# A scheduled attention and MoE kernel: one operand of the weight conversion moves to PSUM, three small steps change engine, the planner gets other costs

## The chip, the core and the metric

The kernel runs on one core of one Trainium2 chip, in one launch. The metric is the device time of one execution in microseconds (us). Engines are named as in the profile: PE is TensorE, DVE VectorE, ACT ScalarE, POOL GpSimd, SP the SyncE queue that issues the DMAs.

## What is computed

Three steps in a row, in float32 (the weights arrive as float64):

```python
for t in range(S):                     # gated linear attention, B=4, H=8, S=768, D=48
    state = alpha[:, :, t, :, None] * state + einsum('bhd,bhe->bhde', k[:, :, t], v[:, :, t])
    y[:, :, t] = einsum('bhd,bhde->bhe', q[:, :, t], state)
x = y.transpose(0, 2, 1, 3).reshape(3072, 384)
h = x @ w_in                           # 384 -> 2048
g = (a0 + a1*h + a2*h**2 + a3*h**3) / (1 + |b0|*|h| + |b1|*h**2 + 1e-6)
x = g @ w_out                          # 2048 -> 384
s = x @ w_gate                         # 384 -> 1536
out = (s / (1 + exp(-s)) * (x @ w_val)) @ w_out2
```

## The kernel before, in words

**Stages.** Attention goes over 24 chunks of 128 time steps (`attention`). For a chunk PE transposes alpha, k and q (aT, kT, qT), DVE runs two scans along time over alpha (bb forward, cc backward, lines 666 and 674) and makes kt and qt from them (682, 692), PE makes the scores sc, ACT copies them to aa and POOL masks them (715). PE transposes kt back (kn), and forms the state's update upd and the output yT from aa, v and the carried state st_s. The state st_c is then multiplied by bC, the products of alpha at the chunk's end (678, 781, 783), and ACT copies it into st_s (788). The result goes to DRAM (xd).

The first MoE (`moe1`) takes 512 tokens at a time and 16 slices f of w_in and w_out. A slice is an **h group** of nine matmuls, a chain over ACT, POOL and DVE (lines 863 to 893) that ends in gg, and nine second matmuls into acc. t2, an affine function of |h|, has two lines: 867 for ACT and 869 for DVE. The second MoE (`moe2`) takes 384 tokens and 12 slices: gate pg, value pv, their product pp, and the output matmuls po. Each float32 product is three fp32r matmuls of a high part and a low part.

**Conversion.** Each of the 68 weight slices arrives as two 32-bit words per number (`split_`). DVE shifts the upper word (line 550, result e), joins the sign to it (556, result x), ACT scales the lower word (578) and copies x to the high part (580), POOL adds the lower word (583) and subtracts the high part (531). The slices 1 to 6 of a fixed list do the last steps on DVE (564 to 574). e and a later temporary share one SBUF tile.

**Order.** Nothing of the order stands in the code: each step is given to `Plan.op` with a due time, one or two engines with a cost in us, what it reads and writes, and a mark for DVE steps that the planner keeps apart from POOL's. `Plan.order` plays the plan through, in cost and due time, and the instructions are issued in the order that comes out. A step with two engines gets the second one only where the plan is late by more than a threshold:

```python
            if c[2]:
                r = max(r, c[0] + late - THETA)
```

PSUM has eight banks, which the planner hands out; three belong to the accumulators, the others to h, the transposes (tr), attention's scores and outputs (att), and the gate and value groups (g). While an h group holds one:

```python
                    if held["h"] + held["tr"] + held["att"] + held["g"] + len(t) > 5:
                        return 1e9
```

An h bank is held until line 889 has read it, since the chain writes intermediate results back into it.

Of the kernel before, what the change touches and what calls it, by code (L numbers as in the profile page):

```python
# [19 lines left out]
PE, DVE, ACT, POOL, DMA = range(5)  # L20
CAPS = {"w": 99, "early": 9, "att": 3, "h": 5, "acc": 3, "g": 4, "tr": 1}
HOP = {PE: 0.22, DVE: 0.2, ACT: 0.2, POOL: 0.15, DMA: 2.1}
SAME = {PE: 0.0, DVE: 0.07, ACT: 0.09, POOL: 0.05, DMA: 2.1}
THETA = 4.46

# [9 lines left out]
class Plan:  # L35
# [51 lines left out]
    def order(self):  # L87
# [46 lines left out]
        def ready(e, c):  # L134
            r = c[3]
            if c[2]:
                r = max(r, c[0] + late - THETA)
            if e == DVE and c[4]:
                r = max(r, lock[1])
            if e == POOL:  # L140
                r = max(r, lock[0])
            if takes[c[1]]:
                t = takes[c[1]]
                us = units[t[0].cls]
                if len(us) < len(t) or held[t[0].kind] + len(t) > CAPS[t[0].kind]:
                    return 1e9
                if t[0].cls == "bank" and t[0].kind != "acc" and (held["h"] or t[0].kind == "h"):
                    if held["h"] + held["tr"] + held["att"] + held["g"] + len(t) > 5:
                        return 1e9
                r = max(r, sorted(us.values())[len(t) - 1])  # L150
            return r
# [203 lines left out]
def gla_moe_moe2_kernel(  # L355
# [151 lines left out]
    def split_(v, name, src):  # L507
# [18 lines left out]

        plan.op(v - 4.14, [(DMA, 1.1 if wide else 0.6, load)], (), (st,))

        def low(x):
            def f(eng):  # L530
                return lambda: eng.tensor_tensor(w.t[:, 1], x.t, w.t[:, 0].bitcast(F32), ALU.subtract)  # L531

            plan.op(v, ways(0.96, f(nc.gpsimd), 0.47, f(nc.vector)), (x, w), (w,))

        if not wide:
            plan.op(v, [(ACT, 0.42, lambda: nc.scalar.copy(w.t[:, 0], st.t))], (st,), (w,))
            low(st)
            return w
        e = new("stage", [128, DM], F32, "we", 2, name + "_e")
        x = new("stage", [128, DM], F32, "wx", 2, name + "_x")  # L540

        def w0():
            return st.t[:, :, 0]

        def w1():
# [3 lines left out]
            v,  # L549
            [(DVE, 0.27, lambda: nc.vector.tensor_scalar(  # L550
                e.t.bitcast(U32), w1(), 5, 2, ALU.logical_shift_left, ALU.logical_shift_right), True)],
            (st,), (e,),
# [3 lines left out]
            [(DVE, 0.47, lambda: nc.vector.scalar_tensor_tensor(  # L556
                x.t.bitcast(U32), w1(), 0xC0000000, e.t.bitcast(U32), ALU.bitwise_and, ALU.bitwise_or), True)],
            (st, e), (x,),
        )
        if slots_dve[0] <= slots[0] <= slots_dve[1]:  # L560
            plan.op(v, [(ACT, 0.42, lambda: nc.scalar.copy(w.t[:, 0], x.t))], (x,), (w,))
            plan.op(
                v,
                [(DVE, 0.27, lambda: nc.vector.tensor_scalar(
                    e.t.bitcast(U32), x.t.bitcast(U32), 0xFF800000, None, ALU.bitwise_and))],
                (x,), (e,),
            )
            plan.op(
                v,
                [(DVE, 0.47, lambda: nc.vector.scalar_tensor_tensor(  # L570
                    e.t, w0(), 2.0**-52, e.t, ALU.mult, ALU.mult), True)],
                (st, e), (e,),
            )
            plan.op(v, [(DVE, 0.47, lambda: nc.vector.tensor_tensor(x.t, x.t, e.t, ALU.add))], (x, e), (x,))
        else:


            plan.op(v, [(ACT, 0.5, lambda: nc.scalar.activation(e.t.bitcast(U32), w0(), AF.Copy, scale=2.0**-29))],
                    (st,), (e,))
            plan.op(v, [(ACT, 0.42, lambda: nc.scalar.copy(w.t[:, 0], x.t))], (x,), (w,))  # L580
            plan.op(
                v,
                [(POOL, 0.96, lambda: nc.gpsimd.tensor_tensor(
                    x.t.bitcast(U32), x.t.bitcast(U32), e.t.bitcast(U32), ALU.add))],
                (x, e), (x,),
            )
# [43 lines left out]
    def attention(v0, dv, m):  # L630
# [76 lines left out]
        for g in range(2):  # L707
            plan.op(
                v0 + 4 * dv,
                [(ACT, 0.48, lambda g=g: nc.scalar.copy(aa[g].t, quad(sc[g].t)))],  # L710
                (sc[g],), (aa[g],),
            )
            plan.op(
                v0 + 4 * dv,
                [(POOL, 0.6, lambda g=g: nc.gpsimd.affine_select(
                    out=aa[g].t, in_=aa[g].t, pattern=[[0, NP], [1, 128]], compare_op=ALU.is_ge,
                    fill=0.0, base=0, channel_multiplier=-1))],
                (aa[g],), (aa[g],),
            )
# [57 lines left out]
        if first:  # L777
            plan.op(v0 + 6 * dv, [(DVE, 0.27, lambda: nc.vector.tensor_tensor(st_c.t, u4(), bCx(), ALU.mult))],
                    (upd, bC), (st_c,))
        else:  # L780
            plan.op(v0 + 6 * dv, [(DVE, 0.27, lambda: nc.vector.tensor_tensor(st_c.t, u4(), st_c.t, ALU.add))],
                    (upd, st_c), (st_c,))
            plan.op(v0 + 6 * dv, [(DVE, 0.27, lambda: nc.vector.tensor_tensor(st_c.t, st_c.t, bCx(), ALU.mult))],
                    (st_c, bC), (st_c,))
# [53 lines left out]
    def moe1(vs, n, part, f0, f1, xt, win, wout):  # L838
# [4 lines left out]
        def first(f):  # L843
# [9 lines left out]
            def mm1():  # L853
                for j in range(NJ):
# [178 lines left out]
    def moe2(vs, n, f0, f1, yy, wg, wv, wo):  # L1033
# [28 lines left out]
        def second(f, pp):  # L1062
# [167 lines left out]
```

## Time and profile before

| | |
|---|---|
| three runs | 1053.42 to 1054.92 us, median 1054.92 |
| profiled execution: its time, its span | 1056.59 us, 1054.9 us |
| mean granted PE clock | 0.985 of full |
| busy: PE, DVE, ACT, POOL | 1002.8, 841.2, 614.5, 460.4 us |
| HBM traffic over the span | 107 GB/s |

The span is the time from the first instruction to the last; the execution's own time is a little longer. An engine's busy time is the time in which it had an instruction in work; that of a DVE or POOL instruction includes what it waits for a port inside the instruction. PE's matmuls overlap each other, so that the difference of their starts is their price, not their length. Attention lies between 0 and 440 us, the first MoE's h groups between 53 and 573 us, the second MoE behind them.

### The profile page before, as it was taken

The page shows a single profiled execution, that of the slowest core. Times are in us where ns is not written, and L with a number is a line of the kernel's source. Part 1 is how long each engine was busy: PE and PEld are TensorE (multiplying, and loading weights), DVE is VectorE, ACT ScalarE, POOL GpSimd, SP SyncE. Part 2 cuts the span into 40 slices and gives each one's busy share as a digit, 9 for nine tenths or more (in the row PEclk, how much of TensorE's full clock was granted, in tenths as well). Part 3 has the DMA queues.
Part 4 walks back from the last instruction along what each step waited for, and adds up shares of the span by engine and source line. Part 5 has one row for each costly group of instructions (what it writes and reads, how often), then busy time and mean ns, then how long its engine had stood idle before and what let it go on. Part 6 is the DMA issues. An engine that isn't in the chain of part 4 may idle for free.

```text
span 1054.9 us, 16741 instructions
## 1 busy us (share of the span) xinstructions
PE 1002.8 (95%) x5974; PEld 898.5 (85%) x5974; DVE 841.2 (80%) x1570; ACT 614.5 (58%) x1148; POOL 460.4 (44%) x397
## 2 busy tenths in 40 slices
PE   8799889999799999999999999999999999999996
PEld 7677677788578788878887888999999999999996
DVE  7999999999998988987999888659866756565422
ACT  4585687998688988788898665432222213232221
POOL 3365778878785775556787765500000000000000
PEclk9999999999999999999999999999999999999999
DMA  8885754422432222031012454224545444343100
GB/s 187 198 205 130 175 143 113 128 83 76 113 86 80 81 67 81 1 112 44 1 61 61 136 174 148 83 81 130 172 142 166 150 120 152 105 141 106 53 1 26
DMA packets 163883, 113.64 MB, mean 108 GB/s; under 512 B 105040, under 2 KB 141904, under 8 KB 163792
## 3 DMA queue, kind: packets, MB, share of 16 engines
q1 hardware_dynamic: 163792, 112.49, 38.3%
q8 instruction: 49, 0.80, 0.3%
q14 instruction: 42, 0.34, 0.1%
HBM read 95.95 MB, written 16.52 MB: 107 GB/s over the span
## 4 chain that ended last, share of the span: by engine, by line
PE 34%; DVE 9%; ACT 3%; DMA 2%; issue 2%; POOL 0%; DVEq 0%; SPq 0%; ACTq 0%
PE po L1069 4%; PE po L1068 4%; PE po L1067 4%; PE pg L834 4%; PE pv L835 4%; PE pg L836 4%; PE pg L835 4%; PE pv L836 4%; PE pv L834 4%; DVE yy L950 1%; DMA out_dram<-os 1%; DVE h L885 1%; DVE t L883 1%; DMA wg_st<-in_moe_w_gate_dram 1%; DVE t L879 1%
## 5 line engine op out<-in xcount | busy, mean ns | idle before, releaser
L877 POOL TENSOR_TENSOR t<-t,t 128x512 f32<-128x512 f32 x96 | 130.4, 1359 | 70.8 <-ACT t L867 54.9
L804 POOL TENSOR_TENSOR gg<-t,gg 128x512 fp32r<-128x512 f32 x96 | 134.3, 1401 | 55.3 <-ACT gg L893 33.4
L1053 ACT CAST pp<-sg 128x384 fp32r<-128x384 f32 x96 | 49.2, 513 | 176.2 <-DVE sg L1051 169.3
L1051 DVE TENSOR_TENSOR sg<-sg,pv 128x384 f32<-128x384 f32 x96 | 53.0, 552 | 105.0 <-PE pv L836 103.6
L834 PE MATMUL acc<-gg,wout 128*128 128x512 f32 x288 | 117.3, 407 | 4.1 <-DVE ys L924 2.5
L834 PE MATMUL h<-xt,win 128*128 128x512 f32 x288 | 117.0, 406 | 2.8 <-ACT aa L710 2.1
L835 PE MATMUL acc<-gg,wout 128*128 128x512 f32 x288 | 114.9, 399 | 3.6 <-POOL gg L804 3.5
L836 PE MATMUL h<-xt,win 128*128 128x512 f32 x288 | 114.0, 396 | 3.4 <-POOL win L531 1.8
L835 PE MATMUL h<-xt,win 128*128 128x512 f32 x288 | 114.0, 396 | 0.1
L836 PE MATMUL acc<-gg,wout 128*128 128x512 f32 x288 | 114.0, 396 | 0.0
L1050 ACT ACTIVATE sg<-pg 128x384 f32<-128x384 f32 x96 | 47.1, 491 | 90.8 <-PE pg L836 89.5
L1069 PE MATMUL po<-wo,pp 128*128 128x384 f32 x288 | 98.4, 342 | 1.6 <-DVE pp L1056 1.6
L1067 PE MATMUL po<-wo,pp 128*128 128x384 f32 x288 | 97.4, 338 | 2.1 <-ACT pp L1053 2.0
L835 PE MATMUL pg<-yy,wg 128*128 128x384 f32 x288 | 97.1, 337 | 0.9 <-DVE yy L950 0.9
L1068 PE MATMUL po<-wo,pp 128*128 128x384 f32 x288 | 97.3, 338 | 0.0
L834 PE MATMUL pg<-yy,wg 128*128 128x384 f32 x288 | 97.1, 337 | 0.0
L836 PE MATMUL pg<-yy,wg 128*128 128x384 f32 x288 | 96.9, 337 | 0.0
L835 PE MATMUL pv<-yy,wv 128*128 128x384 f32 x288 | 96.7, 336 | 0.0
L836 PE MATMUL pv<-yy,wv 128*128 128x384 f32 x288 | 96.5, 335 | 0.0
L834 PE MATMUL pv<-yy,wv 128*128 128x384 f32 x288 | 96.4, 335 | 0.0
L883 DVE SCALAR_TENSOR_TENSOR t<-t,h 128x512 f32<-128x512 f32 x96 | 65.3, 680 | 21.4 <-ACT h L882 17.2
L1056 DVE TENSOR_TENSOR pp<-sg,pp 128x384 fp32r<-128x384 f32 x96 | 60.2, 627 | 26.7 <-ACT pp L1053 25.6
(143 smaller groups left out, 2648.0 us busy)
## 6 DMA issues: line engine op xcount, KB each, us to landing
chk<-in_moe_w_out_dram SPq DMA_DIRECT2D x28, 384.0 KB, 3.3
xr<-xd SPq DMA_DIRECT2D x27, 256.0 KB, 2.8
y1d<-ys SPq DMA_DIRECT2D x27, 256.0 KB, 2.2
win_st<-in_moe_w_in_dram SPq DMA_DIRECT2D x16, 384.0 KB, 3.5
wout_st<-in_moe_w_out_dram SPq DMA_DIRECT2D x16, 384.0 KB, 3.6
chk<-in_moe_w_in_dram SPq DMA_DIRECT2D x16, 384.0 KB, 3.8
nata<-in_alpha_dram SPq DMA_DIRECT2D x24, 192.0 KB, 3.4
natk<-in_k_dram SPq DMA_DIRECT2D x24, 192.0 KB, 3.1
```

The lines of the kernel that those rows point to most:

```text
L804: return lambda: eng.tensor_tensor(out_(), in0(), in1().bitcast(F32), ALU.subtract)
L834: nc.tensor.matmul(out_, wh, xh, start=start, stop=False)
L835: nc.tensor.matmul(out_, wh, xl, start=False, stop=False)
L836: nc.tensor.matmul(out_, wl, xh, start=False, stop=stop)
L877: plan.op(v, [pool(T, lambda: nc.gpsimd.tensor_tensor(t1(), t1(), t2(), ALU.mult))], (b1, b2), (b1,))
L883: plan.op(v, [dve(T, lambda: nc.vector.scalar_tensor_tensor(t1(), t1(), ONE_EPS, h(), ALU.add, ALU.mult))], (b1, hb), (b1,))
L1051: plan.op(v, [(DVE, 0.47, lambda: nc.vector.tensor_tensor(sg.t, sg.t, pv.t[:, 0:TB], ALU.mult))], (sg, pv), (sg,))
L1053: plan.op(v, [(ACT, 0.42, lambda: nc.scalar.copy(pp.t[:, 0], sg.t))], (sg,), (pp,))
L1056: [(DVE, 0.47, lambda: nc.vector.tensor_tensor(pp.t[:, 1], sg.t, pp.t[:, 0].bitcast(F32), ALU.subtract))],
L1067: nc.tensor.matmul(o, pp.t[:, 0, s], w[:, 0], start=f == f0, stop=False)
L1068: nc.tensor.matmul(o, pp.t[:, 0, s], w[:, 1], start=False, stop=False)
L1069: nc.tensor.matmul(o, pp.t[:, 1, s], w[:, 0], start=False, stop=f == f1 - 1)
```

## The change

- The conversion's e moves from SBUF to a PSUM bank of a new kind, cv, of which one may be held at a time and which counts among the five. The later temporary r gets the SBUF tile. Lines 550 and 556 (554 and 560 in the new file) lose the mark that keeps them apart from POOL; two of the steps of slices 1 to 6 get or lose it.
- bC is copied by ACT; the state's product with bC goes to POOL; the second engine for t2 is POOL for DVE.
- The planner's costs, biases, due times and threshold get other values (DMA of a weight 1.5 for 1.1, POOL's steps some 4% more, the output matmuls' due time 5.98 for 4.32 behind the gate group, an attention chunk PA 7.59 for 6.93 and others). The order of all engines comes out anew.

```diff
-CAPS = {"w": 99, "early": 9, "att": 3, "h": 5, "acc": 3, "g": 4, "tr": 1}
+CAPS = {"w": 99, "early": 9, "att": 3, "h": 5, "acc": 3, "g": 4, "tr": 1, "cv": 1}
-THETA = 4.46
+THETA = 3.82
...
-                    if held["h"] + held["tr"] + held["att"] + held["g"] + len(t) > 5:
+                    if held["h"] + held["tr"] + held["att"] + held["g"] + held["cv"] + len(t) > 5:
...
-        e = new("stage", [128, DM], F32, "we", 2, name + "_e")
+        e = bank("cv", name + "_e")
+        r = new("stage", [128, DM], F32, "we", 2, name + "_r")
...
-            [(DVE, 0.27, lambda: nc.vector.tensor_scalar(
-                e.t.bitcast(U32), w1(), 5, 2, ALU.logical_shift_left, ALU.logical_shift_right), True)],
+            [(DVE, 0.45, lambda: nc.vector.tensor_scalar(
+                ex().bitcast(U32), w1(), 5, 2, ALU.logical_shift_left, ALU.logical_shift_right))],
...
-                x.t.bitcast(U32), w1(), 0xC0000000, e.t.bitcast(U32), ALU.bitwise_and, ALU.bitwise_or), True)],
+                x.t.bitcast(U32), w1(), 0xC0000000, ex().bitcast(U32), ALU.bitwise_and, ALU.bitwise_or))],
...
-        plan.op(v0, [(DVE, 0.08, lambda: nc.vector.tensor_copy(bC.t, bb.t[:, C:L:C1]))], (bb,), (bC,))
+        plan.op(v0, [(ACT, 0.1, lambda: nc.scalar.copy(bC.t, bb.t[:, C:L:C1]))], (bb,), (bC,))
...
-            plan.op(v0 + 6 * dv, [(DVE, 0.27, lambda: nc.vector.tensor_tensor(st_c.t, st_c.t, bCx(), ALU.mult))],
+            plan.op(v0 + 6 * dv, [(POOL, 0.57, lambda: nc.gpsimd.tensor_tensor(st_c.t, st_c.t, bCx(), ALU.mult))],
...
-                    (DVE, 0.19 + T / 1920, lambda: nc.vector.tensor_scalar(
+                    (POOL, 0.17 + T * 0.001, lambda: nc.gpsimd.tensor_scalar(
                         t2(), t1(), absb[:, 1:2], absb[:, 0:1], ALU.mult, ALU.add)),
...
-            plan.op(vs[f - f0] + 4.32, [(PE, 1.56, mm4)], (wo[f], pp), tuple(po))
+            plan.op(vs[f - f0] + 5.98, [(PE, 1.56, mm4)], (wo[f], pp), tuple(po))
...
-    plan.bias = {"w": -2.95, "att": 12.49, "x": 0.54, "moe": -2.36}
+    plan.bias = {"w": -4.13, "att": 12.34, "x": -0.20, "moe": -2.25}
```

Counted over the program, DVE loses 24 copies of bC, 16 state products, 24 instructions t2, 3 of line 531 and 1 of line 804; ACT gains the 24 copies and 10 of t2; POOL gains the 16 products, 14 of t2, the 3 and the 1. PE's matmuls are the same in number.

**What moves: DVE in the first 50 us.** One chunk of attention on DVE before, between the qt of the fifth and of the sixth chunk, behind bC's copy and a step of the conversion's tail; win and wout are slices of weights under conversion.

```order
L550 TENSOR_SCALAR wout_e<-wout_st 128x384
L570 SCALAR_TENSOR_TENSOR win_e<-win_st,win_e 128x384
L666 SCALAR_TENSOR_TENSOR bb<-al,seed_f 128x516
L574 TENSOR_TENSOR win_x<-win_x,win_e 128x384
L670 RECIPROCAL seed_r<-bb 128x4
L531 TENSOR_TENSOR win_566<-win_x,win_566 128x384
L674 SCALAR_TENSOR_TENSOR cc<-al,seed_r 128x516
L781 TENSOR_TENSOR st_c<-upd,st_c 128x192
L556 SCALAR_TENSOR_TENSOR wout_x<-wout_st,wout_e 128x384
L783 TENSOR_TENSOR st_c<-st_c,bC 128x192
L682 TENSOR_TENSOR kt<-kT,cc 128x512
L692 TENSOR_TENSOR qt<-qT,bb 128x512
```

The same place in the changed program:

```order
L554 TENSOR_SCALAR win_e<-win_st 128x384
L560 SCALAR_TENSOR_TENSOR win_x<-win_st,win_e 128x384
L670 SCALAR_TENSOR_TENSOR bb<-al,seed_f 128x516
L568 TENSOR_SCALAR win_r<-win_x 128x384
L674 RECIPROCAL seed_r<-bb 128x4
L574 SCALAR_TENSOR_TENSOR win_r<-win_st,win_r 128x384
L678 SCALAR_TENSOR_TENSOR cc<-al,seed_r 128x516
L785 TENSOR_TENSOR st_c<-upd,st_c 128x192
L578 TENSOR_TENSOR win_x<-win_x,win_r 128x384
L686 TENSOR_TENSOR kt<-kT,cc 128x512
L696 TENSOR_TENSOR qt<-qT,bb 128x512
```

The two first steps of a conversion now follow each other at once, the state's product and bC's copy are gone from DVE, and the slice under conversion here is one that comes earlier in the list.

**What moves: DVE around wo0, a slice of the second MoE's weights.** wo0's e before, written and read within 17 rows, here the piece with the writing (numbers behind the names tell buffers apart):

```order
L885 SCALAR_TENSOR_TENSOR h_5573<-t4_5608,prm_88,h_5573 128x512
L878 TENSOR_TENSOR t4_5666<-t4_5666,h_5615 128x512
L889 SCALAR_TENSOR_TENSOR t4_5608<-t1_5605,h_5573 128x512
L879 SCALAR_TENSOR_TENSOR t4_5666<-t4_5666,prm_88,h_5615 128x512
L550 TENSOR_SCALAR wo0_e_5702<-wo0_st_3551 128x384
L550 TENSOR_SCALAR wg1_e_5706<-wg1_st_3808 128x384
L883 SCALAR_TENSOR_TENSOR t1_5646<-t1_5646,h_5615 128x512
```

In the changed program, on DVE, its writing, while the 21st chunk of attention is begun:

```order
L560 SCALAR_TENSOR_TENSOR wv0_x_3481<-wv0_st_3256,wv0_e_3471 128x384
L889 SCALAR_TENSOR_TENSOR h_3348<-t4_3395,prm_88,h_3348 128x512
L554 TENSOR_SCALAR wo0_e_3496<-wo0_st_3362 128x384
L893 SCALAR_TENSOR_TENSOR t4_3395<-t1_3393,h_3348 128x512
L882 TENSOR_TENSOR t4_3498<-t4_3498,h_3422 128x512
L883 SCALAR_TENSOR_TENSOR t4_3498<-t4_3498,prm_88,h_3422 128x512
L670 SCALAR_TENSOR_TENSOR bb_3543<-al_117,seed_f_118 128x516
```

And its reading, 282 rows later on the same engine:

```order
L893 SCALAR_TENSOR_TENSOR t4_5625<-t1_5617,h_5589 128x512
L887 SCALAR_TENSOR_TENSOR t1_5637<-t1_5637,h_5606 128x512
L560 SCALAR_TENSOR_TENSOR wo0_x_5704<-wo0_st_3362,wo0_e_3496 128x384
L889 SCALAR_TENSOR_TENSOR h_5606<-t4_5647,prm_88,h_5606 128x512
L882 TENSOR_TENSOR t4_5702<-t4_5702,h_5649 128x512
```

wo0's e is written far earlier than before, and sits in its PSUM bank from there to the reading; between the two stand the last four chunks of attention and 43 executions of line 893.

**What moves: POOL in the attention stretches.** Before, behind the tenth h group:

```order
L715 AFFINE_SELECT aa_1063<-aa_1063 128x512
L715 AFFINE_SELECT aa_1067<-aa_1067 128x512
L804 TENSOR_TENSOR gg<-t_938,gg 128x512
L877 TENSOR_TENSOR t_1039<-t_1039,t_1081 128x512
L804 TENSOR_TENSOR xt<-xr,xt 128x512
L804 TENSOR_TENSOR gg<-t_981,gg 128x512
L715 AFFINE_SELECT aa_1196<-aa_1196 128x512
```

The changed program on POOL, at about the same chunk:

```order
L787 TENSOR_TENSOR st_c<-st_c,bC 128x192
L719 AFFINE_SELECT aa_1050<-aa_1050 128x512
L719 AFFINE_SELECT aa_1054<-aa_1054 128x512
L808 TENSOR_TENSOR gg<-t_899,gg 128x512
L587 TENSOR_TENSOR win_x<-win_x,win_r 128x384
L787 TENSOR_TENSOR st_c<-st_c,bC 128x192
L531 TENSOR_TENSOR win_1023<-win_x,win_1023 128x384
L719 AFFINE_SELECT aa_1176<-aa_1176 128x512
```

The state's products (787) stand in POOL's queue among the masks, the weights' additions and the subtractions for gg.

## Rows read from the trace of the kernel before

**Rows 1.** The page, part 1: span; busy us (share), instructions

```profile
PE 1002.8 (95%) x5974; PEld 898.5 (85%) x5974; DVE 841.2 (80%) x1570; ACT 614.5 (58%) x1148; POOL 460.4 (44%) x397
```

**Rows 2.** Busy by stretch: stretch, length; PE, PEld, DVE, ACT, POOL; PEclk, DMA share, GB/s

```profile
0.00:53.00 53.00, 43.43 (x481) 38.08 (x481) 45.06 (x81) 26.19 (x52) 16.63 (x33) 1.00 0.85 192
53.00:171.00 118.00, 105.61 (x866) 84.96 (x863) 112.02 (x167) 87.15 (x166) 81.14 (x67) 0.97 0.65 159
171.00:300.00 129.00, 118.50 (x678) 96.16 (x679) 119.70 (x182) 106.81 (x195) 104.42 (x86) 0.96 0.39 103
300.00:578.00 278.00, 272.68 (x1334) 223.07 (x1333) 253.28 (x380) 239.75 (x413) 188.49 (x150) 0.99 0.19 58
578.00:700.00 122.00, 116.44 (x634) 111.32 (x633) 93.17 (x139) 67.37 (x147) 69.70 (x62) 0.99 0.42 131
700.00:1046.00 346.00, 345.87 (x1990) 344.94 (x1988) 217.38 (x624) 87.00 (x178) 0.00 (x0) 1.00 0.37 112
```

**Rows 3.** PE's waits: waiting group <- releaser: us in total, times, longest (two of 23 groups)

```profile
PE sc L701 <- DVE qt L692: 11.4, 8, 3.7
...
PE h L834 <- DVE ys L924: 0.7, 1, 0.7
```

**Rows 4.** Timeline of DVE, 262 to 279 us: start, length, instruction

```profile
262.54 0.55 DVE L556 SCALAR_TENSOR_TENSOR win_x<-win_st,win_e 128x384 uint32<-128x384 uint32 x1
263.01 0.35 DVE L550 TENSOR_SCALAR wout_e<-wout_st 128x384 uint32<-128x384 uint32 x1
...
275.95 1.55 DVE L556 SCALAR_TENSOR_TENSOR wout_x<-wout_st,wout_e 128x384 uint32<-128x384 uint32 x1
...
278.03 0.68 DVE L692 TENSOR_TENSOR qt<-qT,bb 128x512 f32<-128x512 f32 x1
```

**Rows 5.** Timeline of POOL in the same stretch

```profile
274.97 2.12 POOL L877 TENSOR_TENSOR t<-t,t 128x512 f32<-128x512 f32 x1 [0.80 <-ACT t L867]
```

**Rows 6.** Timeline of PE in the same stretch

```profile
278.76 1.16 PE L701 MATMUL sc<-qt,kt 48*128 48x128 f32 x16 [3.67 <-DVE qt L692]
```

**Rows 7.** Busy time of DVE in lines 550 and 556 alone, whole span

```profile
0.00:1055.00 1055.00, 42.84 (x68) 0.99 0.39 108
...
0.00:1055.00 1055.00, 57.12 (x68) 0.99 0.39 108
```

**Rows 8.** Groups by line, DVE: count; busy, mean ns; idle before, releaser

```profile
L869 DVE TENSOR_SCALAR t<-t,absb 128x512 f32<-128x512 f32 x24 | 18.9, 788 | 1.0 <-ACT t L863 1.0
...
L783 DVE TENSOR_TENSOR st_c<-st_c,bC 128x192 f32<-128x192 f32 x16 | 10.4, 648 | 0.1
L678 DVE COPY bC<-bb 128x4 f32<-128x4 f32 x24 | 10.1, 420 | 0.0
...
L781 DVE TENSOR_TENSOR st_c<-upd,st_c 128x192 f32<-128x192 f32 x16 | 5.5, 346 | 0.0
...
L1104 DVE COPY os<-po 128x384 f32<-128x384 f32 x2 | 1.1, 558 | 4.7 <-DMA out_dram<-os 2.8 <-PE po L1069 1.9
```

**Rows 9.** Groups by line, POOL and ACT

```profile
L877 POOL TENSOR_TENSOR t<-t,t 128x512 f32<-128x512 f32 x96 | 130.4, 1359 | 70.8 <-ACT t L867 54.9 <-DVE t L869 10.4 <-PE acc L836 3.0
...
L867 ACT ACTIVATE t<-t,absb 128x512 f32<-128x512 f32 x72 | 58.8, 816 | 0.3
...
L628 ACT ACTIVATE absb<-prm 128x2 f32<-128x2 f32 x1 | 0.2, 203 | 0.0
```

**Rows 10.** Timeline of PE and DVE: first and last h group, line 889

```profile
52.98 0.48 PE L834 MATMUL h<-xt,win 128*128 128x512 f32 x1
...
67.12 0.68 DVE L889 SCALAR_TENSOR_TENSOR t<-t,h 128x512 f32<-128x512 f32 x1
...
570.49 0.39 PE L834 MATMUL h<-xt,win 128*128 128x512 f32 x1
...
572.31 0.39 PE L836 MATMUL h<-xt,win 128*128 128x512 f32 x1
...
586.10 0.69 DVE L889 SCALAR_TENSOR_TENSOR t<-t,h 128x512 f32<-128x512 f32 x1
```

More of the change, by code (lines that the diff above doesn't have):

```diff
@@ L525, in load @@
             nc.sync.dma_start(dst, src)
-        plan.op(v - 4.14, [(DMA, 1.1 if wide else 0.6, load)], (), (st,))
+        plan.op(v - 4.14, [(DMA, 1.5 if wide else 0.6, load)], (), (st,))
         def low(x):
@@ L531, in f @@
                 return lambda: eng.tensor_tensor(w.t[:, 1], x.t, w.t[:, 0].bitcast(F32), ALU.subtract)
-            plan.op(v, ways(0.96, f(nc.gpsimd), 0.47, f(nc.vector)), (x, w), (w,))
+            plan.op(v, ways(1.0, f(nc.gpsimd), 0.47, f(nc.vector)), (x, w), (w,))
         if not wide:
@@ L538, in split_, with ex @@
             return w
-        e = new("stage", [128, DM], F32, "we", 2, name + "_e")
+        e = bank("cv", name + "_e")
+        r = new("stage", [128, DM], F32, "we", 2, name + "_r")
         x = new("stage", [128, DM], F32, "wx", 2, name + "_x")
+        def ex():
+            return e.t[:, 0:DM]
         def w0():
@@ L564, in split_ @@
                 [(DVE, 0.27, lambda: nc.vector.tensor_scalar(
-                    e.t.bitcast(U32), x.t.bitcast(U32), 0xFF800000, None, ALU.bitwise_and))],
-                (x,), (e,),
+                    r.t.bitcast(U32), x.t.bitcast(U32), 0xFF800000, None, ALU.bitwise_and), True)],
+                (x,), (r,),
             )
@@ L570, in split_ @@
                 [(DVE, 0.47, lambda: nc.vector.scalar_tensor_tensor(
-                    e.t, w0(), 2.0**-52, e.t, ALU.mult, ALU.mult), True)],
-                (st, e), (e,),
+                    r.t, w0(), 2.0**-52, r.t, ALU.mult, ALU.mult), True)],
+                (st, r), (r,),
             )
-            plan.op(v, [(DVE, 0.47, lambda: nc.vector.tensor_tensor(x.t, x.t, e.t, ALU.add))], (x, e), (x,))
+            plan.op(v, [(DVE, 0.47, lambda: nc.vector.tensor_tensor(x.t, x.t, r.t, ALU.add), True)], (x, r), (x,))
         else:
-            plan.op(v, [(ACT, 0.5, lambda: nc.scalar.activation(e.t.bitcast(U32), w0(), AF.Copy, scale=2.0**-29))],
-                    (st,), (e,))
+            plan.op(v, [(ACT, 0.5, lambda: nc.scalar.activation(r.t.bitcast(U32), w0(), AF.Copy, scale=2.0**-29))],
+                    (st,), (r,))
             plan.op(v, [(ACT, 0.42, lambda: nc.scalar.copy(w.t[:, 0], x.t))], (x,), (w,))
@@ L582, in split_ @@
                 v,
-                [(POOL, 0.96, lambda: nc.gpsimd.tensor_tensor(
-                    x.t.bitcast(U32), x.t.bitcast(U32), e.t.bitcast(U32), ALU.add))],
-                (x, e), (x,),
+                [(POOL, 1.0, lambda: nc.gpsimd.tensor_tensor(
+                    x.t.bitcast(U32), x.t.bitcast(U32), r.t.bitcast(U32), ALU.add))],
+                (x, r), (x,),
             )
@@ L714, in attention @@
                 v0 + 4 * dv,
-                [(POOL, 0.6, lambda g=g: nc.gpsimd.affine_select(
+                [(POOL, 0.63, lambda g=g: nc.gpsimd.affine_select(
                     out=aa[g].t, in_=aa[g].t, pattern=[[0, NP], [1, 128]], compare_op=ALU.is_ge,
@@ L799, in pool @@
     def pool(T, f):
-        return (POOL, 0.17 + T * 0.0021, f)
+        return (POOL, 0.2 + T * 0.0021, f)
     def sub(T, out_, in0, in1):
@@ L1107, in moe2 @@
             plan.op(vl, [(DMA, 0.6, lambda os=os, r0=r0: nc.sync.dma_start(out[r0 : r0 + 128, :], os.t))], (os,), ())
-    PA, P2 = 6.93, 4.68
-    MM2 = 16.88
+    PA, P2 = 7.59, 4.68
+    MM2 = 16.91
     def segments(nf, spec):
@@ L1129, in gla_moe_moe2_kernel @@
         at.append(at[-1] + p * (f1 - f0))
-    s0 = 36.60
-    LEADM = 40.47
+    s0 = 36.44
+    LEADM = 52.57
     done = HEAD[1] / C
-    cv = [3.50 + 6.78 * m for m in range(HEAD[1] // C)]
+    cv = [3.50 + 6.65 * m for m in range(HEAD[1] // C)]
     start, vs = [], []
@@ L1143, in gla_moe_moe2_kernel @@
             while len(cv) < int(done + c + 1e-6):
-                cv.append(max(t - 19.88, cv[-1] + 6.59))
+                cv.append(max(t - 19.98, cv[-1] + 6.03))
             done += c
@@ L1170, in gla_moe_moe2_kernel @@
     segs2 = segments(F2, "0:0-2 1:0-2 2:0-2 3:0-2 0:2-6 1:2-6 2:2-6 3:2-6 0:6-12 1:6-12 2:6-12 3:6-12 4 5 6 7")
-    t, vs2 = end_a + 7.96, []
+    t, vs2 = end_a + 9.57, []
     for n, part, f0, f1 in segs2:
```

## The prediction

> **What bounds the kernel now.** I read the page's busy shares first [rows 1]: TensorE (PE) is busy for 1002.8 us of the 1054.9 us span, so work can at most be pushed into some 52 us of PE idle time and into what the clock costs. The table by stretches says where these lie [rows 2]; the reader is to compare, in each row, PE's busy time with the length, and look at VectorE (DVE) and the granted clock beside it. PE idles 9.6 us of the first 53, 12.4 of the next 118, 10.5 of the next 129, 5.3 of the next 278, 5.6 of the next 122. In the second and third row DVE is busy 95% and 93% of the time, and the clock averages 0.97 and 0.96: at half clock (1.2 for 2.4 GHz) in about 7 us and 10 us, of which half, 3.5 and 5.2 us, is lost; 2.8 and 1.2 us follow in the fourth and fifth. From 700 us on PE is busy 345.87 of 346 us: nothing can be had there, and the last 9 us are the store. In all 43.4 us idle and 12.7 us of clock, all before 700 us.
>
> Next, PE's waits by releaser [rows 3]. DVE is named for 21.0 us, in 8 groups from the scores' wait for qt, 11.4 us, down to the h groups' wait for ys, 0.7 us; that is about half of the 43.4 us. So DVE is the engine to relieve, in the attention stretches above all.
>
> Then why DVE is full. At 263.01 and 262.54 us the two first steps of a weight's conversion take 0.35 and 0.55 us; at 275.95 the second step takes 1.55 us on the same shape [rows 4]. Beside it GpSimd (POOL) runs from 274.97 to 277.09 [rows 5], and the long row ends 0.41 us after POOL does, nearly its undisturbed length: a DVE step that reads two SBUF tensors waits POOL's instruction out. Behind it lies qt, at 278.03, and for qt PE waited 3.67 us [rows 4, 6], its longest wait.
>
> **What the change does to DVE.**
>
> Conversion, 68 weights: the first step (line 550) is busy 42.84 us, the second (line 556) 57.12 us [rows 7], together 99.96. With e in PSUM the second has one SBUF input only. That such an instruction escapes POOL is in the trace: st_c's sum, which reads PSUM, takes 346 ns, its product with bC, same shape, all in SBUF, 648 ns [rows 8]. So the second step costs its short 0.55 us. For the first step no row shows a PSUM output: below, the 0.35 us it takes undisturbed [rows 4], above, the 558 ns of DVE's copy of the same 384 elements out of PSUM [rows 8]. I take 0.55, since that row has PSUM at one end. 68 x 1.10 = 74.8 us: **25.2 us less**. At the lower end of the first step, 68 x 0.90 = 61.2, it is 38.8 less; if both steps go on waiting and the first is 0.2 us slower besides, it is 13.6 *more*.
> The Trainium skill, "VectorE: DVE Perf Modes", section "Why PSUM operands drop a tier", says that an fp32 instruction with an operand in PSUM runs one element at a time. By this rule the first step takes the upper end, by the undisturbed row the lower; the sum goes by the upper.
>
> bC, 24 copies: 10.1 us leave DVE [rows 8]; on ScalarE (ACT) each costs about 0.2 us, as the nearest small ACT row, 203 ns [rows 9]: 4.9 us. The next chunk's scan now waits for an ACT copy, but it waits for al on the same in-order queue already, and where bC stands behind al, it is 0.2 us.
>
> State product, 16: 10.4 us leave DVE [rows 8]. POOL has no row of 192 elements; its product of 512 takes 1359 ns [rows 9]. Scaled by size, 0.5 us, unscaled 1.36; I take 0.65, 10.4 us. In DVE's order the product stood up to two rows behind the sum; it now starts on an engine that is 31% busy early (16.63 of 53 us) [rows 2]. The ACT copies st_s wait for it, and behind them kn and PE's update.
>
> Late t2, 24 on DVE: 18.9 us leave [rows 8]. By the order 14 go to POOL (at 0.79, DVE's own time, to 1.36 us: 11 to 19 us) and 10 to ACT (816 ns each: 8.2 us) [rows 9]. Three more subtractions of weights and one of x go from DVE to POOL: about 3 us.
>
> Sum for DVE: 25.2 + 10.1 + 10.4 + 18.9 + 3 = **67.6 us of 841.2 less**. POOL gains some 27 us, ACT 13; in the third stretch, the fullest for both, POOL is busy 104.4 of 129 us and ACT 106.8 [rows 2], so both have room, and I cost what they gain at nothing; if POOL's queue had none, its 27 us would stand behind gg and aa (rival D).
>
> **What of it reaches the end.** PE's matmuls are the same in number and form, chunks and h groups stand at nearly the same places (chunk 17's scores behind 12 h groups for 13, chunk 20's behind 35 for 32), so a stretch shortens by PE's loss at most. The losses add up to 43.4 + 12.7 = 56.1 us, less than DVE's relief; 31.6 of them (12.4 + 3.5 + 10.5 + 5.2) lie in the two stretches where DVE is full, 24.5 in the three others. DVE is named for half of PE's waits, 21.0 of 43.4 us; those on ACT and POOL shrink only where these waited for DVE themselves. In the two full stretches I take a little over half, 17 us; in the others, where DVE is busy 85, 91 and 76%, somewhat over a third, 9 us (in the last of them the later place of the output matmuls, 5.98 for 4.32 in their due times, also gives pp more time). Together **26 us**.
>
> Against it stands one bank. The order shows wo0's e written while chunk 21 is being prepared and read 282 DVE rows later; in between lie some 43 h groups, and h and attention have four banks for five. An h group plus a second-matmul group take PE 18 x 0.2275 = 4.1 us (nine starts from 570.49 to 572.31 [rows 10]). An h bank is held from the group's first matmul to line 889: 52.98 to 67.80 us for the first h, 570.49 to 586.79 for the last [rows 10], 14.8 and 16.3 us. Four banks at 4.1 us allow 16.4. That is just enough, and a DVE with less to do shortens it; a few chunks of attention squeeze in between. I charge 3 us.
>
> Net 23 us. The profiled execution took 1056.59 us for a span of 1054.9; less 23 it is 1033.6. The median of the three runs, 1054.92, lies 0.16% lower, so the forecast is **1032 us**.
>
> **Rivals.**
>
> *A, slower: the bank.* If h keeps its bank 18.6 us in that stretch, four banks give an h group every 4.65 us for 4.1: 43 x 0.55 = 24 us; four chunks of attention, which need eight short tenancies each (1.5 us, a guess at PE's group and the copy that empties it), take 48 bank-us, 12 us of four. Together 36, less the 23 + 3 of gain: some 1065 us. It decides from about 17.7 us of holding on, where 43 x 0.33 + 12 use up the 26. Against it: 14.8 and 16.3 us were measured with DVE over 90% busy, and the planner counts the bank when it sets the order. 0.12.
>
> *B: the wait is not released*, or the first step in PSUM is slower than 0.56 us. Then conversion gives nothing and only the moved steps count, 42.4 of 67.6 us: 26 x 0.63 = 16, less 3: 1042 us. Against it speak 346 and 648 ns [rows 8]. 0.13.
> The Trainium skill, "SBUF — State Buffer", section "Who interferes with whom", says that a DVE instruction with at most one SBUF input, outside its two-port modes, does not contend with GpSimd. By that rule B falls; the trace agrees, 346 against 648 ns, and so its chance is small.
>
> *C: the relief is used almost fully*, because ACT's and POOL's waits were DVE's at second hand (kn behind st_s behind st_c): all 31.6 us in the full stretches and half of the 24.5 elsewhere, 44 less 3: 1014 us. 0.08.
>
> *D: nothing arrives.* The planner's order was shifted everywhere, and the PE loss is inherent in the switches between groups, or POOL's longer queue (27 us) hands it to gg and aa: 1053 to 1057. 0.06.
>
> **How the numbers follow.** Forecast (1016 to 1048 us) 0.61, A 0.12, B 0.13, C 0.08, D 0.06. A measurement of this kernel tells 0.2%, 2 us, from no change. Faster: 0.61 + 0.13 + 0.08 = 0.82; within 0.2%: 0.05, most of D; slower: 0.13, A and the rest of D. The range takes in the forecast, B and the edge of C: 1012 to 1053; A and most of D lie above.
>
> **What would show it.** Right: line 554 at 0.47 to 0.56 us and line 560 at 0.55 us in all 68 rows, no long ones; DVE's total near 774 us; in 53 to 300 us PE's waits for qt cut by more than half and the clock at 0.98 or above; first gate matmul some 18 to 22 us earlier than before; from there on the same length less 3 us. Wrong: h matmuls that wait for line 893 between chunk 21 and the 81st h group (A); long rows of 560 beside POOL (B); PE's waits named POOL or ACT as long as DVE's were (D).

## The result and the profile after

Four runs of the changed kernel took 1037.14 to 1039.63 us, median 1038.13, beside 1053.42 to 1054.92 us for the kernel before, median 1054.62. The ratio is 0.9847, with an interval of 0.983 to 0.9864: **16.5 us faster**. The forecast was 1032 us in 1012 to 1053. The profiled execution took 1037.14 us for a span of 1035.4 us, with a mean granted clock of 0.992. One of the twelve executions of e2 below took 1230.37 us and is left out of its median here (with it the median is 1053.66, 15.5 us more than the change, as e11's expectation has it).

Part 1 of the page after, busy us, share and instructions, to be set against [rows 1]:

```profile
PE 993.4 (96%) x5974; PEld 891.0 (86%) x5974; DVE 773.6 (75%) x1502; ACT 623.6 (60%) x1182; POOL 466.2 (45%) x431
```

DVE lost 67.6 us, the sum of the prediction to the tenth. POOL gained 5.8 us where some 27 were put on it; the last section says why.

The changed steps: first the table by stretches narrowed to line 554 and to line 560 over the whole span (columns as in [rows 7]), then two groups of POOL and one of ACT (columns as in [rows 8]).

```profile
0.00:1055.00 1055.00, 37.60 (x68) 0.99 0.39 108
...
0.00:1055.00 1055.00, 37.26 (x68) 0.99 0.39 108
...
L787 POOL TENSOR_TENSOR st_c<-st_c,bC 128x192 f32<-128x192 f32 x16 | 11.3, 707 | 19.4 <-DVE st_c L785 19.4
L873 POOL TENSOR_SCALAR t<-t,absb 128x512 f32<-128x512 f32 x14 | 10.9, 775 | 6.5 <-ACT t L867 6.2 <-ACT h L886 0.3
...
L682 ACT COPY bC<-bb 128x4 f32<-128x4 f32 x24 | 4.8, 199 | 3.1 <-DVE bb L670 3.0
```

All 68 rows of line 554 last 0.54 to 0.56 us and all 68 of line 560 0.52 to 0.56: the long rows [rows 4] are gone. The two come to 74.9 us; 74.8 were predicted. A state product costs 707 ns for the 650 assumed, a copy of bC 199 for 200.

The table by stretches (columns as in [rows 2]), first five rows:

```profile
0.00:53.00 53.00, 46.53 (x493) 40.95 (x493) 43.86 (x71) 27.84 (x61) 18.96 (x37) 0.97 0.86 191
53.00:171.00 118.00, 112.17 (x957) 90.88 (x956) 109.69 (x168) 100.62 (x202) 92.37 (x87) 1.00 0.72 175
171.00:300.00 129.00, 123.78 (x697) 99.26 (x695) 112.48 (x179) 117.88 (x216) 106.88 (x95) 1.00 0.38 105
300.00:578.00 278.00, 264.83 (x1280) 216.63 (x1279) 221.00 (x347) 235.78 (x408) 195.00 (x165) 0.99 0.20 57
578.00:700.00 122.00, 119.06 (x677) 116.86 (x676) 83.93 (x158) 60.59 (x134) 53.02 (x49) 1.00 0.42 133
```

Length less PE's busy time gives PE's idle time. In the first three stretches it fell from 9.6, 12.4 and 10.5 us to 6.5, 5.8 and 5.2; in the second and third the clock rose from 0.97 and 0.96 to 1.00, while in the first it fell from 1.00 to 0.97. In the fourth idle time *rose*, from 5.3 to 13.2 us, and something was given back there. PE's waits by releaser (columns as in [rows 3]) say by whom:

```profile
PE h L838 <- ACT al L663: 3.3, 2, 2.6
...
PE h L838 <- ACT ys L922: 2.1, 1, 2.1
...
PE h L838 <- DVE wv_x L560: 1.5, 1, 1.5
PE sc L705 <- DVE qt L696: 1.5, 1, 1.5
```

The scores' wait for qt fell from 11.4 us [rows 3] to 1.5. New is `h <- DVE wv_x L560`: an h matmul waits for a conversion's second step, which reads the cv bank. That bank has entered PE's path.

How long it is held shows in DVE's timeline of lines 554 and 560, summed up by tile (count; shortest, median and longest in ns; start of the first and the last). In each pair the first starts are wo0's, its write and its read. Of the kernel after:

```profile
L554 DVE TENSOR_SCALAR wo_e<-wo_st x12: 547/554/561, 272.5 to 632.1; 128x384 uint32<-128x384 uint32 x12
...
L560 DVE SCALAR_TENSOR_TENSOR wo_x<-wo_st,wo_e x12: 541/548/555, 507.2 to 633.4; 128x384 uint32<-128x384 uint32 x12
```

wo0's bank lies still from 272.5 to 507.2 us, 235 us, most of the stretch in which PE's idle time rose. PE idles 9.6 us in it, and all of this is in the same table of waits, cut to these 235 us:

```profile
PE acc L838 <- DVE t L893: 4.1, 2, 3.0
PE acc L838 <- DVE ys L928: 2.1, 1, 2.1
PE h L838 <- DVE ys L928: 1.4, 1, 1.4
PE kT L655 <- DVE t L893: 0.8, 1, 0.8
PE h L838 <- ACT al L663: 0.7, 1, 0.7
PE aT L655 <- DVE ys L928: 0.6, 1, 0.6
```

None of these matmuls reads what the releaser writes: an h matmul reads xt and win, a second matmul gg and wout, a transpose its input. What line 893, the additions into ys and the copy al have in common is that each is the last reader of a bank. So every one of these waits is for a PSUM bank, under the name of whoever held it last.

Set against the kernel before, chunk 17's scores start 15.6 us earlier (155.61 for 171.23), the 32nd h group 17.0 (250.0 for 267.0), the 48th 22.2 (328.9 for 351.1), the 96th only 11.6 (558.9 for 570.5) and the first gate matmul 12.8 (565.01 for 577.85). From there to the last po matmul it takes 461.6 us for 468.1. So 22 us were won by the middle of the first MoE, about 10 were lost between its 48th and 96th group, and 6.5 were won in the second MoE.

### The profile page after: what moved, and what is told of

The parts are those of the page before. It is cut to its first block, busy times and chain, and to the rows that moved or that the text cites. A ratio compares the mean times of both kernels' runs of the same rounds, so it can differ in the third digit from the quotient of the medians.

```text
span 1035.4 us, 16697 instructions
## 1 busy us (share of the span) xinstructions
PE 993.4 (96%) x5974; PEld 891.0 (86%) x5974; DVE 773.6 (75%) x1502; ACT 623.6 (60%) x1182; POOL 466.2 (45%) x431
## 4 chain that ended last, share of the span: by engine, by line
PE 43%; ACT 3%; DVE 3%; DMA 2%; issue 1%; POOL 0%; DVEq 0%; ACTq 0%
PE po L1071 4%; PE po L1073 4%; PE po L1072 4%; PE pv L838 4%; PE pg L839 4%; PE pg L838 4%; PE pv L840 4%; PE pg L840 4%; PE pv L839 4%; PE acc L839 1%; PE acc L838 1%; PE acc L840 1%; DVE yy L954 1%; ACT t L885 1%; DMA wo_st<-in_moe_w_out_dram 1%
## 5 line engine op out<-in xcount | busy, mean ns | idle before, releaser
L808 POOL TENSOR_TENSOR gg<-t,gg 128x512 fp32r<-128x512 f32 x96 | 128.7, 1341 | 48.4 <-ACT gg L897 32.7
L881 POOL TENSOR_TENSOR t<-t,t 128x512 f32<-128x512 f32 x96 | 125.5, 1307 | 51.7 <-ACT t L871 46.6
L838 PE MATMUL h<-xt,win 128*128 128x512 f32 x288 | 116.0, 403 | 8.9 <-ACT al L663 3.3
L840 PE MATMUL h<-xt,win 128*128 128x512 f32 x288 | 112.5, 391 | 0.2 <-DVE win L531 0.2
L839 PE MATMUL h<-xt,win 128*128 128x512 f32 x288 | 112.4, 390 | 0.0
L887 DVE SCALAR_TENSOR_TENSOR t<-t,h 128x512 f32<-128x512 f32 x96 | 65.3, 681 | 35.6 <-ACT h L886 33.8
L882 DVE TENSOR_TENSOR t<-t,h 128x512 f32<-128x512 f32 x96 | 65.4, 682 | 32.8 <-ACT t L878 29.1
```

Of the source, the lines that this page charges most:

```text
L808: return lambda: eng.tensor_tensor(out_(), in0(), in1().bitcast(F32), ALU.subtract)
L838: nc.tensor.matmul(out_, wh, xh, start=start, stop=False)
L839: nc.tensor.matmul(out_, wh, xl, start=False, stop=False)
L840: nc.tensor.matmul(out_, wl, xh, start=False, stop=stop)
L881: plan.op(v, [pool(T, lambda: nc.gpsimd.tensor_tensor(t1(), t1(), t2(), ALU.mult))], (b1, b2), (b1,))
L882: plan.op(v, [dve(T, lambda: nc.vector.tensor_tensor(t4(), t4(), h(), ALU.mult))], (b4, hb), (b4,))
```

## The experiments

The theory after the result: DVE's relief is what brought the gain, and the held bank is what gave part of it back. The rivals: the new order alone did it; the relief was worth nothing at the end; planned and real costs have to agree. All kernels compute the whole result. e1, e3 and e10 write the same e twice, which changes no value. Line numbers are those of the changed file. "Ratio" is to the kernel before, with its interval; 1038.1 is the median of the kernel after.

**e1: the order of the change, the first step twice.**

```diff
-            [(DVE, 0.45, lambda: nc.vector.tensor_scalar(
+            [(DVE, 0.45, lambda: [nc.vector.tensor_scalar(
...
+                ...) for _ in range(2)])],
```

> The changed kernel in its own order, engine by engine, except that VectorE runs the first step of each of the 68 conversions (line 554) twice: 68 more instructions of about 0.47 us from start to start, 32 us on VectorE, somewhat more than the 26 us that conversion lost by the change. Theory (VectorE's relief makes the gain): PE waits for VectorE again in the attention stretches, and 0.2 to 0.35 us of time come with each us on VectorE: 1045 to 1050 us. Rival (the new order of the planner makes the gain, VectorE has slack to spare): within 2 us of 1038.

Measured 1061.82 us, ratio 1.007 (1.0053 to 1.0088), 23.7 more than the change. DVE's busy time rose by 34.0 us, to 807.6: 0.70 us lost for each. The relief matters, and far more than expected.

**e2: the order of the change, the moved steps issued on DVE again** (bC, state product, late t2).

```diff
-(ACT, 0.1, lambda: nc.scalar.copy(bC.t, ...
+(ACT, 0.1, lambda: nc.vector.tensor_copy(bC.t, ...
-(POOL, 0.57, lambda: nc.gpsimd.tensor_tensor(st_c.t, ...
+(POOL, 0.57, lambda: nc.vector.tensor_tensor(st_c.t, ...
-(POOL, 0.17 + T * 0.001, lambda: nc.gpsimd.tensor_scalar(
+(POOL, 0.17 + T * 0.001, lambda: nc.vector.tensor_scalar(
```

> The changed kernel in its own order, but the three steps that changed engine are issued on VectorE again at the same places: bC's 24 copies, the 16 state products, the 14 instructions t2 that stood on GpSimd; the conversion stays in PSUM. VectorE gets about 8 + 9 + 11 = 28 us back (0.34, 0.57 and 0.79 us each), GpSimd loses 22 us. Theory (VectorE's relief): 1043 to 1048 us. Rival (order alone): within 2 us of 1038. Second rival (GpSimd is the tighter engine now, so taking 22 us from it helps): 1033 to 1036.

Measured 1053.32 us, ratio 0.9982 (0.9966 to 0.9997), 15.2 more, for 21.0 us of DVE (794.6): 0.72 each. The expectation was too low again.

**e3: both.**

> Both of the former together, in the changed kernel's order: VectorE is as full as before the change (about 835 us). Theory: the gain is gone, 1051 to 1060 us, that is about the sum of the two single costs. Rival (order alone): within 3 us of 1038. If it comes out well above 1060, the new order leans on a relieved VectorE more than the old one leaned on anything.

Measured 1076.98 us, ratio 1.0211 (1.0192 to 1.023), 38.9 more; e1 and e2 add up to 38.9 as well, and DVE gained 55.0 us (828.6), so 0.71 each. With a DVE that is 12.6 us *less* busy than before, this kernel is 22.4 us slower than before: something beside DVE's load costs some 20 us in the changed program.

**e4: the bank is not taken early.** The first step may be issued only when its reader's output buffer x is free, so that the reader can follow. The order is planned anew; the longest way from line 554 to its 560 falls from some 280 DVE rows to 6.

```diff
                 ex().bitcast(U32), w1(), 5, 2, ALU.logical_shift_left, ALU.logical_shift_right))],
-            (st,), (e,),
+            (st,), (e,), tuple(x.before),
```

> The changed kernel, except that a conversion's first step may not be issued before the buffer of x, its second step's result, is free; so no bank waits for a buffer: the longest distance between the two steps falls from 280 VectorE rows to 6. The planner orders everything anew for it. Theory (wo0's e kept one of five banks from chunk 21 to the 81st h group, and that is why PE idles 13.2 us between 300 and 578 us for 5.3 before): PE's idle time in that stretch falls by 4 to 8 us and the time to 1031 to 1035. Rival (these waits belong to the changes of accumulators and to y's additions, and the bank costs nothing): within 2 us of 1038, with the same idle time there.

Measured **1018.98 us**, ratio 0.9665 (0.9648 to 0.9682): 19.2 less than the change, the fastest of all. DVE's busy time is 766.0 us. Its fourth stretch (columns as above):

```profile
300.00:578.00 278.00, 273.29 (x1349) 226.71 (x1348) 225.66 (x358) 235.59 (x415) 207.75 (x175) 1.00 0.23 69
```

PE's idle time there is 4.7 us for 13.2, at a clock of 1.00, with DVE 5 us *busier* in the stretch. From the 48th to the 96th h group it takes 211.8 us for 230.0 in the change, but with two chunks of attention in between for three, so these two stretches don't hold the same work; e9 below gives the like comparison. By this run the bank's charge was not 3 us.

**e8 and e9: which holds.** e8 has the rule for wo0 alone (longest way then 30 rows); e9 for all but wo0, which keeps its bank over 266 rows while the others fall to 6 or less.

```diff
-            (st,), (e,),
+            (st,), (e,), tuple(x.before) if name == "wo0" else (),
```

In e9 the same line has `!=`.

> The changed kernel, planned anew with one rule for one weight: wo0's first step may not be issued before its x buffer is free. The other 67 conversions are as in the change; the longest distance between the two steps falls from 280 VectorE rows to 30. Theory (the one long hold of a PSUM bank by wo0's e costs the changed kernel some 19 us): 1017 to 1025 us, as with the rule for all 68 (1018.98). Rival (that run was fast because its order was drawn anew, or because the many short holds got shorter): 1030 to 1042 us.

> The mirror of it: the rule for all weights but wo0, so that wo0's e alone still sits in its bank, for 266 VectorE rows, and all other distances are 6 or less. Theory (wo0's hold is the cost): 1033 to 1042 us, close to the changed kernel. Rival (new order, or the short holds): 1017 to 1026 us.

e8 took 1028.74 us (ratio 0.9755, 0.9729 to 0.9781), e9 1028.26 (0.9753, 0.973 to 0.9776). Neither expectation was met, in opposite senses: I had put nearly all on wo0. Freeing it gives 9.4 us (change to e8) or 9.3 (e9 to e4); the rule for the others gives 9.9 (change to e9) or 9.8 (e8 to e4). The four totals are additive within 0.1 us; as each is known to some 2 or 3 us, that closeness is in part chance.

The rule also leaves DVE lighter: 765.0 us in e9 and 766.0 in e4, for 773.6 in the change and 771.9 in e8. At 0.7 us for each us of DVE (e1 to e3) this alone would make 6.0 of the 9.9 us and 4.1 of the 9.8, an estimate. wo0's 9.3 and 9.4 stand between runs whose DVE is nearly equal.

In e9, which differs from e4 by wo0's rule alone, wo0's write and read, the fourth stretch, PE's waits while wo0's bank is held (280.0 to 501.1 us) and the longest of them in PE's timeline:

```profile
L554 DVE TENSOR_SCALAR wo_e<-wo_st x12: 549/555/564, 280.0 to 623.1; 128x384 uint32<-128x384 uint32 x12
...
L560 DVE SCALAR_TENSOR_TENSOR wo_x<-wo_st,wo_e x12: 542/552/556, 501.1 to 623.8; 128x384 uint32<-128x384 uint32 x12
```

```profile
300.00:578.00 278.00, 265.02 (x1316) 218.97 (x1315) 220.60 (x350) 232.50 (x407) 201.98 (x176) 0.98 0.23 67
```

```profile
PE h L838 <- DVE t L893: 5.6, 2, 4.6
PE acc L838 <- DVE ys L928: 2.9, 1, 2.9
PE h L838 <- DVE ys L928: 1.2, 1, 1.2
```

```profile
395.78 0.79 PE L838 MATMUL h<-xt,win 128*128 128x512 f32 x1 [4.62 <-DVE t L893]
```

And of e4, PE's waits in the same 280.0 to 501.1 us (two of five groups) and the same pair of wo0:

```profile
PE acc L838 <- DVE ys L928: 0.9, 2, 0.6
...
PE h L838 <- DVE t L893: 0.3, 1, 0.3
```

```profile
L554 DVE TENSOR_SCALAR wo_e<-wo_st x12: 544/548/555, 488.3 to 622.6; 128x384 uint32<-128x384 uint32 x12
...
L560 DVE SCALAR_TENSOR_TENSOR wo_x<-wo_st,wo_e x12: 541/548/556, 489.4 to 623.3; 128x384 uint32<-128x384 uint32 x12
```

With wo0's bank held, h matmuls wait for line 893, the line that frees an h bank, for 5.6 us, one of them 4.62 us at 395.78; with the bank taken for 1.1 us (488.3 to 489.4) it is 0.3 us in the same window. That is rival A's mechanism. The two runs hold the same work from the 48th to the 96th h group, two chunks of attention included, and here is that stretch (columns as in [rows 2]), first of e9, then of e4:

```profile
329.30:552.51 223.21, 210.23 (x983) 171.55 (x981) 178.33 (x279) 190.12 (x327) 163.77 (x140) 0.98 0.19 57
```

```profile
330.89:542.71 211.82, 207.11 (x980) 168.13 (x979) 174.84 (x275) 185.70 (x320) 154.70 (x130) 1.00 0.19 56
```

With the bank held it takes 11.4 us more: 8.3 of PE's idle time (13.0 for 4.7) and 3.1 of PE's busy time, at a granted clock of 0.98 for 1.00. So wo0's price lies in this stretch. The fourth stretch's PE idle time is 13.0 us in e9 and 13.2 in the change, 6.4 in e8 (PE busy 271.60) and 4.7 in e4.

**e10: the first step twice, and the planner told so** (0.92 for 0.45 us).

> The kernel with the first step run twice (1061.82 us in the changed kernel's order), but the planner is told its cost, 0.92 us for 0.45, and orders anew. Theory (VectorE's 32 us themselves cost the time): 1053 to 1063 us. Rival (what costs is that the planned and the real cost of a step differ, so that in-order queues stand wrong; the title's times as traced are the gain): 1038 to 1047 us.

Measured 1065.19 us, ratio 1.0103 (1.0079 to 1.0127). Against e1 the known cost gains nothing (1061.82). So e1's loss is not the mismatch between the plan and the chip; that rival falls.

**e6: the steps of before, all of the planner's new numbers.** Of the kernel before, e in SBUF and the moved steps back in their places; thresholds, due times, biases and costs of the unchanged steps as in the change.

```diff
-THETA = 4.46
+THETA = 3.82
...
-    plan.bias = {"w": -2.95, "att": 12.49, "x": 0.54, "moe": -2.36}
+    plan.bias = {"w": -4.13, "att": 12.34, "x": -0.20, "moe": -2.25}
```

> The kernel before, all its steps on their old engines and e in SBUF, with all the planner's numbers of the change (threshold, biases, due times, GpSimd's and DMA's costs). Theory (the steps carry the gain; VectorE stays as full as before): 1048 to 1062 us. Rival (the numbers carry it): 1030 to 1044 us.

Measured 1058.4 us, ratio 1.0036 (1.0018 to 1.0054), as expected: by themselves the numbers make it 3.8 us slower. PE's idle time in the fourth stretch is 12.9 us here (busy 265.07) with no bank to hold, so that stretch's idle time alone, where DVE is busier (826.8 us in all), does not prove a held bank; e9 against e4, with DVE equal (765.0 and 766.0), does. DVE is 14.4 us less busy here than in the kernel before: at 0.7 that should have given back some 10 us, an estimate, so the new numbers cost more than the 3.8 shows, by something other than DVE's load.

**e5: the changed steps, the planner's numbers of before** (e6's diff the other way round).

> The changed steps (e in PSUM, bC on ScalarE, state product and late t2 on GpSimd) with the planner's numbers of before: threshold, biases, due times, and GpSimd's and DMA's costs. wo0's e is held here too, for 333 VectorE rows. Theory (the steps carry the gain, the numbers little): 1032 to 1045 us. Rival (the numbers carry it): 1048 to 1060 us.

Measured 1052.71 us, ratio 0.9984 (0.9966 to 1.0002): far above the expectation, with a DVE as light as in the change (771.9 us). wo0's hold is longer, 333 rows, and PE's waits of e5 begin:

```profile
PE h L838 <- DVE t L893: 7.1, 7, 1.5
PE h L838 <- DVE kt L686: 4.4, 1, 4.4
```

h matmuls wait for the line that frees their bank here too, in 7 places.

**e12: e5 with the rule of e4** (longest way 9 rows).

> The changed steps with the planner's numbers of before, as in the run that gave 1052.71 us, plus the rule that no conversion's first step is issued before its x buffer is free (longest distance 9 VectorE rows for 333). Theory (the steps are worth some 35 us, and in that run the held bank and the short holds hid most of it): 1025 to 1040 us. Rival (with the old numbers the steps are worth little, with or without a held bank): 1045 to 1054 us.

Measured 1033.14 us, ratio 0.9782 (0.9747 to 0.9817): 19.6 less than e5, the expectation met. The rule is worth as much under either set of numbers (19.6 and 19.2), and here with DVE as busy as without it (771.2 and 771.9 us), so that its gain under these numbers is not DVE's load.

**e11: e4's own order, with e2's edit.**

> The kernel with the rule for all weights (1018.98 us), in its own order, with bC, the state product and the late t2 of GpSimd issued on VectorE again at the same places; e stays in PSUM. In the changed kernel's order that cost 15.5 us. Theory (VectorE's relief, about 0.5 us of time per us of VectorE): 1029 to 1037 us. Rival (without the held bank PE has h groups in reserve and hides VectorE's steps): 1019 to 1024 us.

Measured 1036.44 us, ratio 0.9828 (0.9797 to 0.9859), as expected: 17.5 more than e4, for 25.9 us of DVE (791.9), 0.68 each. As far as these medians tell, DVE's price is the same with and without held banks.

## Why the prediction was right, and which terms were not

The forecast's side and its range were right; its two terms were both too small, and their errors partly cancelled. That 1038 lies so near 1032 is luck to that extent: with the relief as measured and the bank as charged the forecast would have been 1022, with the bank as measured and the relief as charged 1048.

**What bounds the kernel** stood: PE's waits named DVE, and when DVE lost 67.6 us, PE's idle time in the first three stretches fell by 15.0 us (32.5 to 17.5) and the clock there came back to 1.00 where it had been 0.97 and 0.96.

**The costs on DVE** came out: 74.9 us for the two steps (74.8 predicted, at the upper end for the first step, where the row with PSUM at one end was chosen), 773.6 us for DVE in all. ACT's copies and POOL's products cost what the nearest rows said; a t2 on POOL took 775 ns, just under the low end of the 0.79 to 1.36 us given. Rival B falls with 68 short rows, D with 16.5 us.

**"Together 26 us" was too small.** Without the early-taken banks the change is worth 1054.6 - 1019.0 = 35.6 us. I had shared out PE's losses stretch by stretch and taken about half, 26 for 67.6 us of DVE, 0.38 each. The runs near the changed program give 0.68 to 0.72 for each us of DVE (e1, e2, e3, e11). Rival C, which took the relief almost fully at 44 us, was a little nearer in this term. The slope is not the whole account either: e4's DVE is 75.2 us lighter than before, and 35.6 for these is 0.47 each; that the new numbers cost something (e6) accounts for a part of the difference, the rest is open. What lay behind the term was partly seen: the attention chunks and the MoE's chains are queued on DVE one behind the other, so an added us there mostly reaches PE, also in stretches where DVE is busy under 90%.

**"I charge 3 us" was the larger error.** That conversions may take the bank long before their reader can run costs the change 19.2 us (1038.1 to 1019.0 by e4, 1052.7 to 1033.1 by e12; the order drawn anew is in both), of which wo0 costs 9.3 to 9.4. The step took 14.8 and 16.3 us, the holds of the first and the last h group, neither of which lies in the stretch, for what every h group holds its bank, and an even pace. In the change the 49th to the 80th h group hold theirs 9.2 to 26.8 us, 14.9 in the mean (first matmul to the end of line 893; 10.5 to 30.4 and 15.3 before, where none of the five banks was taken for long): the mean is below the 16.4 that four banks allow, as reckoned, but single groups are far above it, and PE idles where a bank comes late, 9.6 us during wo0's hold. (Between wo0's write and its read stand 48 executions of line 893, not 43.) The prediction also looked at the longest hold only; the rule for the other slices, whose ways are much shorter, is worth another 9.9 us. Rival A had the mechanism right, at 36 us, too high.

**The sum with the measured terms:** 1054.6 + 3.8 for the numbers (e6) + 19.2 for the banks; then the relief. That gives 1077.6, and e3, which holds the banks as the change does and whose DVE is as busy as e6's (828.6 and 826.8 us), stands at 1077.0. From there 55.0 us of DVE give back 38.9, and the change stands at 1038.1. Of this only the meeting of 1077.6 and 1077.0 is a check, and it joins runs of different orders; the last step is e3 read backwards.

**The signs given:** rows of 554 and 560, DVE's total, qt's wait (cut by 9.9 of 11.4 us) and the clock came as written. The first gate matmul came 12.8 us earlier, not 18 to 22: 22.2 us were won up to the 48th h group, and 10.6 lost again under wo0's hold. The rest was shorter by 6.5 us, not 3. The sign for A, h matmuls that wait for line 893, was drawn too narrowly: in the change's own trace the `h` waits name al, ys and wv_x, and 893 is named by `acc` and `kT`, but all of them are waits for a bank. Only e9 and e5 show it plainly by that name.

**Open.** In e4, e8, e9 and e12 the planner draws the whole order anew, so their differences hold the bank and the new order together. That 19.2 comes back as 19.6 under other numbers speaks for the bank, and for wo0 the stretch of e9 and e4 with the same work and the waits in it do; a run that moves wo0's write alone, in the change's order, was not made. For the 9.9 us of the other slices short holds, DVE's lighter load and the redrawn order were not told apart. One place of theirs is in the traces: in the change an h matmul waits 2.64 us at 181.29 for the bank that al's copy frees, inside the hold of a slice of wout (158.6 to 183.2 us); e8, which keeps that hold, waits 2.70 us at 181.27, while in e9 and e4, which don't, no wait of an h matmul near there is over 0.7. Nor is it settled why the steps with the numbers of before are worth 21.5 us without holds (1054.6 to 1033.1), and with the new numbers 39.4 (e6 to e4, 1058.4 to 1019.0). The runs come from four sets, in which the kernel before had medians of 1053.8 to 1055.2 us, so that differences of 1 or 2 us between sets say nothing.

## What to carry to other kernels

Moving one operand of a long-waiting DVE instruction to PSUM removed its wait for GpSimd here, in all 68 rows, and the price could be read from rows beforehand; but a scratch bank counts from its writing to its reading, so make the writer wait until the reader can follow (one line here, 19 us with the order it brings). A planner that asks only whether a bank is free when it is taken doesn't see what a tenant that stays costs those who come later: search a new order for the ways between writer and reader, the long and the middling ones. Reckon banks by the spread of their holds, not by the mean, and read a wait for a bank by what the waiting instruction does not read: its releaser has many names. An engine that stands in every chain can be priced by repeating one of its instructions in an unchanged order; sharing out idle time gave 0.38 here, the repetition 0.70, and the change as a whole 0.47 without the early-taken banks, so the slope near one order is an upper guide and not the worth of a new one.

## What the runs showed of the hardware that was not expected

POOL was given some 27 us of work and its busy time rose by 5.8, for the most part because its own rows became shorter. Two groups of the kernel before, then the same lines after (columns as in [rows 8]):

```profile
L804 POOL TENSOR_TENSOR gg<-t,gg 128x512 fp32r<-128x512 f32 x96 | 134.3, 1401 | 55.3 <-ACT gg L893 33.4 <-issue 16.0 <-DVE t L878 2.2
...
L715 POOL TENSOR_SCALAR_AFFINE_SELECT aa<-aa 128x512 f32<-128x512 f32 x48 | 41.1, 878 | 45.4 <-ACT aa L710 45.3
```

```profile
L808 POOL TENSOR_TENSOR gg<-t,gg 128x512 fp32r<-128x512 f32 x96 | 128.7, 1341 | 48.4 <-ACT gg L897 32.7 <-issue 11.2 <-POOL t L881 2.7
L881 POOL TENSOR_TENSOR t<-t,t 128x512 f32<-128x512 f32 x96 | 125.5, 1307 | 51.7 <-ACT t L871 46.6 <-PE acc L840 4.0 <-ACT bC L682 0.3
L719 POOL TENSOR_SCALAR_AFFINE_SELECT aa<-aa 128x512 f32<-128x512 f32 x48 | 35.2, 757 | 32.7 <-ACT aa L714 32.6
```

The products of gg went from 1401 to 1341 ns, those of line 881 from 1359 [rows 9] to 1307, the masks from 878 to 757: 16.5 us over these three lines. In the kernel before, the rows of these three lines that overlap one of the conversion's two first steps (20, 18 and 17 rows) average 1474, 1485 and 1027 ns, the others 1382, 1330 and 796; in the kernel after, those that overlap one average 1304, 1305 and 700, the others 1352, 1307 and 780. So the waiting had gone both ways: beside those DVE steps POOL's rows had been longer too, and with e in PSUM they no longer are. The steps that changed engine are not the reason: in e2, where they stand on DVE again, the three lines average 1344, 1319 and 768 ns.
